# Moving the convolution of one group and the loads of its x to other bundles of a fused convolution and channel-mix kernel

## The chip, the cores and the metric

The kernel runs on one core of a Trainium2 chip. The metric is the device time of one launch in microseconds, as a median of several runs. A profile is one further execution, recorded by the hardware.

## What is computed

A lightweight convolution over time is followed by an RWKV channel mix. With batch 8, sequence 4160, width 192, 8 heads of 24 channels, 7 taps and hidden width 1024:

```python
w = softmax(weight, axis=-1)                                  # 8 heads x 7 taps
y[b, t, h*24 + c] = sum_k w[h, k] * x_pad[b, t + k, h*24 + c] # 6 zero rows ahead of x
y_prev = y shifted by one row
xk = mu_k * y + (1 - mu_k) * y_prev
xr = mu_r * y + (1 - mu_r) * y_prev
k = relu(xk @ w_k)                                            # 192 -> 1024
v = (k * k) @ w_v                                             # 1024 -> 192
out = sigmoid(xr @ w_r) * v
```

## The kernel before

**Work units.** The eight batches are taken as four pairs. A pair's 4160 rows are cut into steps of 512 rows (some of 256), and a step's first product, 192 to 1024, into slots. Four slots make a bundle. There are 260 slots and 65 bundles, 0 to 64. Pair 0 has bundles 0 to 15, pair 1 has 16 to 31, pair 2 (the third) 32 to 47, pair 3 the rest. A full step takes two bundles.

**A bundle** (`bundle_rest`, L938) writes out by hand what each engine does. TensorE computes four slots of k (`k_mm`, L593, 6 matmuls each), one r product (L650, 12 matmuls) and one v product (L681, 64 matmuls in two halves). ScalarE does a relu for each slot (L605) and a sigmoid (L661). VectorE squares the four slots (L619), multiplies r and v (L697), and makes the mixes of a later step (`diff` L536, `scale` L567, `add_y` L573). Where the bundle has a convolution unit, it comes after the fourth slot of k and before the second half of v.

**The convolution** is done ahead of the steps that need it, in groups of rows. Groups 0 to 7 belong to pairs 0 and 1. Groups 8 to 12 are "sparse": 20 blocks of 4 x 26 rows, 2080 rows, of two batches. Group 8 is the second half of pair 1, group 9 the first half of pair 2, groups 10, 11, 12 follow. A sparse group passes through these stages:

- `x_tile` and `load_x`: x goes from HBM into tile `xb`, cast to bf16, by DMAs from the GpSimd (POOL) queue, one batch at a time. The first batch goes in one bundle and the second in a later one, at the bundle's beginning (table `early`). A batch of group 9 is 4 DMAs of L154 and a small one of L148. A write of one word by VectorE (L125 in `x_tile`, L113 in `tie_x`) goes ahead of each batch and ties the load to its place. `x_tile` of group 9 also has one GpSimd memset (L127). `xb` has two buffers: group 9 takes the one of groups 6 and 7, which were convolved in bundles 7, 9, 11 and 12.
- `conv_sparse` (L350): four units, one for each two heads. A unit takes two tiles from the PSUM ring, runs 32 matmuls (L364), and ScalarE casts the two tiles into the two halves of `y` (L337), in 2 instructions for units 0 and 3 and in 4 for units 1 and 2.
- `y_write` (L466): 8 DMAs from the SP queue write `y` to `y_dram` at the end of the bundle of the last unit. `y` has two buffers and a sparse group uses both, so the casts of the next sparse group wait until these 8 DMAs have landed.
- `y_read` (L488): transposing DMAs from the SP queue bring `y_dram` into `yT`, which the mixes read. SP also issues the output stores (L705), two a bundle, and works through all of this in program order.

**The PSUM ring** has four tiles, shared by the k, r and v products and the convolution. A bundle without a unit takes six tiles and one with a unit takes eight.

**Where each group's stages stand** is worked out from `fb`, the bundle in which its rows are first needed, with exceptions in two small dictionaries (L752 and L760). Before the change, around the place in question:

| group | fb | x loaded in | convolved in | y written at the end of | y read at the end of |
|---|---|---|---|---|---|
| 7 | 20 | 7 | 11, 11, 12, 12 | 12 | 15 |
| 8 | 24 | 9, 12 | 14, 15, 16, 17 | 17 | 19, 22 |
| 9 | 32 | 17, 18 | 22, 23, 24, 25 | 25 | 27, 30 |
| 10 | 40 | 24, 25 | 27, 29, 31, 33 | 33 | 35, 38 |
| 11 | 48 | 29, 32 | 35, 37, 39, 41 | 41 | 43, 46 |
| 12 | 56 | 37, 40 | 43, 45, 47, 49 | 49 | 51, 54 |

Of the kernel before, what the change touches and what calls it, by code (L numbers as in the profile page):

```python
# [14 lines left out]
def kernel(  # L15
# [719 lines left out]
    def at(table, b, fn, *a):  # L735
        table.setdefault(b, []).append((fn, a))
# [7 lines left out]
    for g, (p, base, nb, fb, on_pe) in enumerate(groups):  # L744
        if g < 3:
            continue
        if p == 0:
            xs = {3: [1, 1], 4: [2, 2, 3, 3], 5: [4, 4, 5, 5]}[g]
        elif g not in sparse:
            xs = [fb - 9] * 2 + [fb - 7 - (g == 7)] * 2  # L750
        else:
            xs = {8: [14, 15, 16, 17], 9: [22, 23, 24, 25]}.get(g, [fb - 13, fb - 11, fb - 9, fb - 7])  # L752
        for i, b in enumerate(xs):
            xt.setdefault(b, []).append((g, i))
        if not on_pe:
            at(late, xs[-1], y_write, g)
        if g in sparse:
            at(late, max(fb - 5, xs[-1] + 2), y_read, g, slice(0, 1), 2)
            at(late, fb - 2, y_read, g, slice(1, 2), 2)
            b, b1 = {8: (9, 12), 9: (17, 18), 10: (24, 25)}.get(g, (fb - 19, fb - 16))  # L760
            at(early, b, x_tile, g)
            at(early, b, load_x, g, (0,))
            b = b1
            at(early, b, tie_x, g, 1)
            at(early, b, load_x, g, (1,))
            continue
        if not on_pe:
            if g == 4:
                at(mix_c, 4, y_read, g, slice(0, 1), 2)
                at(late, 4, y_read, g, slice(1, 2), 2)  # L770
            else:
                at(late, {5: 6, 6: 11, 7: 15}[g], y_read, g)
        if g > 4:

            b = {5: 1, 6: 3, 7: 7}.get(g)
            b = first_bundle[first_step[p]] + (-15, -11, -7, -3)[(g - 6) % 4] if b is None else b
            table = {5: mix_a, 7: mix_c}.get(g, early)
            at(table, b, x_tile, g)
            at(table, b, load_x, g)
    for s, (p, t0, L, n0, ns) in enumerate(steps):  # L780
        fb = first_bundle[s]
# [27 lines left out]
    for s, j, vb in quads:  # L809
        b = vb - (s == LAST)  # L810
# [261 lines left out]
```

## Time and profile before

| | us |
|---|---|
| median of 3 runs | 411.97 (411.53 to 412.25) |
| the profiled execution | 411.43 |
| its span, first to last instruction | 409.7 |
| around the span | 1.73 |
| granted TensorE clock | 1.0 |

| engine | busy us | share of the span |
|---|---|---|
| TensorE matmul (PE) | 401.9 | 98% |
| TensorE weight load (PEld) | 303.6 | 74% |
| VectorE (DVE) | 371.0 | 91% |
| ScalarE (ACT) | 354.6 | 87% |
| GpSimd (POOL) | 58.8 | 14% |

In what follows a bundle's start is the start of its first k matmul (L593) in the trace. Some of these, in us from the span's start: bundle 15 at 102.19, 16 at 108.53, 17 at 114.87, 18 at 121.18, 19 at 126.90, 22 at 144.10, 25 at 162.96, 27 at 175.02, 38 at 240.94, 43 at 271.25, 51 at 319.05. A window between two starts is the time that the program takes for the bundles between them. An idle time in square brackets names what ended it; "issue" means that the engine waited for nothing that the profile shows.

### The profile page before, as it was taken

To read this page: it belongs to the slowest core of one execution; us is meant where nothing else is said; L and a number is where in the kernel's file an instruction comes from. 1 tells how busy PE (TensorE), PEld (TensorE's weight loads), DVE (VectorE), ACT (ScalarE), POOL (GpSimd) and SP (SyncE) were. 2 spreads that over 40 slices of the span, in tenths; PEclk is the share of its full clock that TensorE was granted. 3 is DMA by queue.
4 is the path that set the end of the run, shared out by engine and by line. 5 is a ranking of instruction groups with operands and counts; after the bars stand their busy time and mean duration, and the time that the engine had idled before them with its cause. 6 is when DMAs were issued, how large, how long until landed. Compare 5 with 4: busy or idle time off the path is not lost.

```text
span 409.7 us, 17419 instructions
## 1 busy us (share of the span) xinstructions
PE 401.9 (98%) x7672; PEld 303.6 (74%) x7672; DVE 371.0 (91%) x672; ACT 354.6 (87%) x426; POOL 58.8 (14%) x91
## 2 busy tenths in 40 slices
PE   8899999999999999999999999999999999999996
PEld 5567767767867777777777777777777778777795
DVE  5899899998989999989999998999999899999973
ACT  6899988898998889998898898889898878877781
POOL 8632022030060004104020012000000002000000
PEclk9999999999999999999999999999999999999999
DMA  9999889997779977998995998979523756221223
GB/s 149 185 199 211 187 192 212 240 190 198 152 106 219 230 219 111 222 239 160 199 164 138 203 205 125 163 187 193 134 78 88 210 136 157 79 70 50 80 78 117
DMA packets 139123, 66.35 MB, mean 162 GB/s; under 512 B 89364, under 2 KB 139048, under 8 KB 139048
## 3 DMA queue, kind: packets, MB, share of 16 engines
q1 hardware_dynamic: 95704, 48.32, 47.2%
q0 software_dynamic: 42544, 16.36, 34.6%
q8 instruction: 60, 0.98, 1.0%
q10 hardware_dynamic: 800, 0.57, 0.5%
q14 instruction: 15, 0.12, 0.1%
HBM read 33.29 MB, written 36.99 MB: 172 GB/s over the span
## 4 chain that ended last, share of the span: by engine, by line
PE 93%; ACT 1%; issue 0%; DVE 0%; ACTq 0%
PE ps_v L681 41%; PE ps_k L593 39%; PE ps_r L650 8%; PE ps_c L364 2%; PE ps_v L633 1%; PE ps_c L319 1%; ACT k_sb L605 1%; ACT y L439 0%; PE ps_c L393 0%; DVE o_sb L717 0%; ACTq L401 0%; ACTq L605 0%
## 5 line engine op out<-in xcount | busy, mean ns | idle before, releaser
L605 ACT ACTIVATE k_sb<-ps_k 128x1024 bf16<-128x1024 f32 x260 | 253.4, 1040 | 34.2 <-PE ps_k L593 33.5
L619 DVE TENSOR_TENSOR k<-k_sb 128x1024 bf16<-128x1024 bf16 x260 | 173.4, 687 | 25.7 <-ACT k_sb L605 25.5
L593 PE MATMUL ps_k<-xk,wk 64*128 64x512 bf16 (+1 forms) x1632 | 191.8, 367 | 1.5 <-DMA wk<-in_moe_w_k_dram 1.4
L681 PE MATMUL ps_v<-wv,k 64*128 64x192 bf16 x4032 | 188.7, 243 | 0.3 <-issue 0.2
L681 PEld LDWEIGHTS <-k 64*128 64x128 bf16 x4032 | 168.6, 94 | 12.8 <-issue 5.1
L593 PEld LDWEIGHTS <-wk 64*128 64x128 bf16 x1632 | 83.8, 94 | 56.3 <-DMA wk<-in_moe_w_k_dram 1.9
L154 POOL DMA_DIRECT2D xb<-in_x_dram x62 | 43.7, 715 | 142.3 <-DVE xb L125 59.2
L697 DVE TENSOR_TENSOR o_sb<-ps_v,r_sb 128x768 f32<-128x768 f32 x64 | 60.8, 951 | 2.6 <-issue 2.4
L661 ACT ACTIVATE r_sb<-ps_r 128x768 bf16<-128x768 f32 x65 | 53.7, 828 | 9.0 <-PE ps_v L681 7.5
L337 ACT CAST y<-ps_c 128x960 bf16<-128x960 f32 (+2 forms) x84 | 52.6, 709 | 0.0
L650 PEld LDWEIGHTS <-xr 64*128 64x128 bf16 x780 | 34.8, 94 | 14.4 <-issue 0.4
L650 PE MATMUL ps_r<-wr,xr 64*128 64x192 bf16 x780 | 43.4, 243 | 0.0
L567 DVE TENSOR_SCALAR xr<-d,mu 128x512 bf16<-128x512 bf16 (+1 forms) x102 | 35.8, 355 | 0.0
L567 DVE TENSOR_SCALAR xk<-d,mu 128x512 bf16<-128x512 bf16 (+1 forms) x99 | 32.5, 359 | 0.1
L536 DVE TENSOR_TENSOR d<-yT 128x1536 bf16<-128x1536 bf16 (+4 forms) x36 | 31.2, 866 | 1.4 <-ACT yT L423 1.4
L573 DVE TENSOR_TENSOR xr<-xr,yT 128x1536 bf16<-128x1536 bf16 (+1 forms) x33 | 31.0, 938 | 1.1
L573 DVE TENSOR_TENSOR xk<-xk,yT 128x1536 bf16<-128x1536 bf16 (+3 forms) x33 | 30.5, 925 | 0.1
L520 POOL COPY y_tail<-yT 128x195 bf16<-128x195 bf16 x4 | 4.4, 1100 | 88.0 <-DMA yT<-y_dram 88.0
L364 PEld LDWEIGHTS <-toe 32*32 32x32 bf16 x640 | 4.4, 87 | 8.6 <-issue 7.4
L364 PE MATMUL ps_c<-xb,toe 32*32 32x240 bf16 x640 | 9.3, 267 | 0.0
L127 POOL MEMSET xb<- 32x384 bf16 x3 | 1.2, 408 | 55.3 <-DVE xb L125 55.3
L413 PE MATMUL ps_t<-toe,xb 128*32 128x120 bf16 (+3 forms) x264 | 5.6, 241 | 0.3 <-ACT xb L247 0.3
(60 smaller groups left out, 66.1 us busy)
## 6 DMA issues: line engine op xcount, KB each, us to landing
out_dram<-o_sb SPq DMA_DIRECT2D x128, 192.0 KB
xb<-in_x_dram POOLq DMA_DIRECT2D x52, 240.0 KB, 8.3
y_dram<-y SPq DMA_DIRECT2D x40, 195.0 KB
y_dram<-y SPq DMA_DIRECT2D x16, 210.0 KB
xb<-in_x_dram POOLq DMA_DIRECT2D x4, 228.0 KB, 4.8
xb<-in_x_dram POOLq DMA_DIRECT2D x4, 192.0 KB, 6.4
wk<-in_moe_w_k_dram POOLq DMA_DIRECT2D x4, 192.0 KB, 6.5
xb<-in_x_dram POOLq DMA_DIRECT2D x2, 216.0 KB, 4.9
```

The lines of the kernel that those rows point to most:

```text
L154: nc.gpsimd.dma_start(out=xb[q0 : q0 + rows, lo:hi, s, :], in_=bass.AP(tensor=x.tensor, offset=x.offset + (b * S + t0 + lo * step) * D, ap ...
L337: nc.scalar.copy(out=bass.AP(tensor=y.tensor, offset=y.offset + d, ap=[y.ap[0], [m * 2 * D, 2], [2 * D, m], [Q, 2], [1, b - a]],), in_=bas ...
L536: nc.vector.tensor_tensor(out=shaped(s, diffs[s][:, cs, :L]), in0=y_of(s, cs, 1), in1=y_of(s, cs, 0), op=ALU.subtract)
L567: nc.vector.tensor_scalar(out=t[:, c, :L], in0=diffs[s][:, c, :L], scalar1=mu[:, i, c : c + 1], scalar2=None, op0=ALU.mult)
L573: nc.vector.tensor_tensor(out=o, in0=o, in1=y_of(s, sl, 0), op=ALU.add)
L593: nc.tensor.matmul(out=ps[:, i, f * L : (f + 1) * L], lhsT=wk[r, c, fs], rhs=xk[r, c, :L], start=c == 0 and f == 0, stop=c == NC - 1 and f ...
L605: nc.scalar.activation(out=k_sb, in_=ps.rearrange("p a b -> p (a b)"), func=AF.Relu)
L619: nc.vector.tensor_tensor(out=o, in0=i, in1=i, op=ALU.mult)
L650: nc.tensor.matmul(out=ps[:, i, k * D : (k + 1) * D], lhsT=xr[q, c, ts], rhs=wr[q, c, :], start=c == 0, stop=c == NC - 1,)
L661: nc.scalar.activation(out=r_sbs[s, j], in_=r_ps.pop((s, j))[:, :, 0 : 2 * D], func=AF.Sigmoid)
L681: nc.tensor.matmul(out=v_ps[s, j][:, bank, k * D : (k + 1) * D], lhsT=k2s[s][q, f, t * P : (t + 1) * P], rhs=wv[q, f, :], start=half == 0 ...
L697: nc.vector.tensor_tensor(out=o_sb.rearrange("p (b t) d -> p b (t d)", b=2), in0=v_ps.pop((s, j)), in1=r_sbs.pop((s, j)), op=ALU.mult,)
```

## The change

Units 0, 1 and 2 of group 9 go from bundles 22, 23, 24 to bundles 19, 21, 23; unit 3 stays in bundle 25. With the exception at L752 gone, the rule `fb - 13, fb - 11, fb - 9, fb - 7` gives 19, 21, 23, 25. The first batch of its x is loaded in bundle 15 instead of 17, the second in bundle 16 instead of 18. Its `y_write` (bundle 25) and its `y_read`s (27 and 30) keep their places, and so does every stage of every other group.

```diff
         else:
-            xs = {8: [14, 15, 16, 17], 9: [22, 23, 24, 25]}.get(g, [fb - 13, fb - 11, fb - 9, fb - 7])
+            xs = {8: [14, 15, 16, 17]}.get(g, [fb - 13, fb - 11, fb - 9, fb - 7])
...
-            b, b1 = {8: (9, 12), 9: (17, 18), 10: (24, 25)}.get(g, (fb - 19, fb - 16))
+            b, b1 = {8: (9, 12), 9: (15, 16), 10: (24, 25)}.get(g, (fb - 19, fb - 16))
             at(early, b, x_tile, g)
             at(early, b, load_x, g, (0,))
             b = b1
             at(early, b, tie_x, g, 1)
             at(early, b, load_x, g, (1,))
```

## The prediction

> **What bounds the kernel.** I read the page's busy shares and the summary of the chain that ended last first, then windows over single bundles.
>
> ```profile
> PE 401.9 (98%) x7672; PEld 303.6 (74%) x7672; DVE 371.0 (91%) x672; ACT 354.6 (87%) x426; POOL 58.8 (14%) x91
> ...
> PE 93%; ACT 1%; issue 0%; DVE 0%; ACTq 0%
> ```
>
> TensorE sets the end. The change adds and removes no matmul, so it can only alter the time that TensorE loses inside its "busy" share. The windows show this. First bundles 19 to 26 (columns: window, length, busy of PE, PEld, DVE, ACT, POOL, clock, DMA share, GB/s):
>
> ```profile
> 126.90:132.63 5.73, 5.73 (x106) 4.35 (x103) 5.28 (x10) 4.58 (x6) 0.00 (x0) 1.00 1.25 227
> ...
> 144.10:150.31 6.21, 6.21 (x138) 4.57 (x134) 6.10 (x10) 5.18 (x7) 0.00 (x0) 1.00 0.58 172
> 150.31:156.64 6.33, 6.33 (x136) 4.58 (x134) 5.67 (x13) 6.33 (x9) 0.29 (x1) 1.00 0.66 167
> 156.64:162.96 6.32, 6.32 (x138) 4.60 (x134) 5.89 (x12) 6.31 (x10) 3.18 (x6) 1.00 1.01 132
> ...
> sum 48.12, PE 48.12 PEld 35.93 DVE 44.51 ACT 43.36 POOL 5.46; mean PE 6.01 PEld 4.49 DVE 5.56 ACT 5.42 POOL 0.68
> ```
>
> A bundle without a unit takes 5.73, the first with one (22) 6.21, the next ones 6.33 and 6.32. In those ACT is busy for the whole bundle: four units in a row make ScalarE the bound. Now bundles 43 to 50, where group 12 has the same four units in every second bundle, as group 9 will have:
>
> ```profile
> 271.25:277.45 6.20, 6.20 (x137) 4.44 (x134) 5.81 (x11) 5.17 (x7) 0.00 (x0) 1.00 0.82 234
> ...
> 289.38:295.14 5.76, 5.76 (x104) 4.39 (x102) 5.29 (x9) 5.72 (x8) 0.00 (x0) 1.00 0.63 151
> ...
> sum 47.80, PE 47.80 PEld 35.58 DVE 44.21 ACT 43.38 POOL 0.00; mean PE 5.97 PEld 4.45 DVE 5.53 ACT 5.42 POOL 0.00
> ```
>
> The timeline of TensorE shows where the difference sits:
>
> ```profile
> 148.62 0.42 PE L364 MATMUL ps_c<-xb,toe 32*32 32x240 bf16 x32
> ...
> 154.81 0.57 PE L364 MATMUL ps_c<-xb,toe 32*32 32x240 bf16 x32
> ```
>
> The same 32 matmuls take 0.42 in bundle 22 and 0.57 in bundle 23, where the late sigmoid holds a tile of the PSUM ring that the unit's second half needs.
>
> **The change, part by part.**
>
> 1. Units 0 to 2 move. The work is the same, so I compare eight bundles with eight: 48.12 before, 47.80 in the pattern that it gets (47.80 also for group 10, bundles 27 to 34). That is **-0.32 us**, of which bundles 23 to 25 give 3 x 0.12 = 0.36 and two bundles after a unit with four casts give 2 x 0.04 back (5.76 for 5.72). Bundle 19 has a unit two bundles after bundle 17, as 27 has after 25 (6.20). The VectorE work of a bundle depends on its parity, and 19, 21, 23 are odd like 27 to 33.
>
> 2. The x loads move two bundles ahead: 10 DMAs, two words written by VectorE (0.06 each) and a memset of POOL (0.41). POOL is idle for 26.94 before the memset, and nothing else stands in its queue between bundles 14 and 17, so its own order costs nothing. The words cost VectorE 0.06 in bundles 15 and 16 and save as much in 17 and 18: nothing. The `xb` buffer has been free since bundle 12. In the trace the loads are issued at 114.58 to 123.36 and the last has landed at 139.34 (by the semaphore updates). Now they are issued some 12.7 us earlier (bundle 15 starts that much before 17), about 102 to 110.5. The slowest last batch was 18.7 us from first issue to landing (120.62 to 139.34), which gives 107.8 + 18.7 = 126.5. Bundle 19's unit needs it at 126.90 + 4.5 = 131.4 (22's began 4.5 after its start). The margin falls to 5 us; without it each late us is an us of TensorE.
>
> 3. What the loads run into. Queue lines (start, duration of the issue):
>
> ```profile
> 104.70 3.85 SPq L488 DMA_TRANSPOSE yT<-y_dram  x1
> ...
> 121.38 7.15 SPq L466 DMA_DIRECT2D y_dram<-y  x8
> ...
> 134.48 7.44 SPq L488 DMA_TRANSPOSE yT<-y_dram  x1
> ```
>
> The read of group 7 (104.70) now lies between the two load batches. Alone it landed 5.8 us after its issue (110.54); group 6's, with a load beside it, took 10.1 (80.51 to 90.56). If both batches went ahead of it, it would land at 126.5, the bound of step 2. Its reader is the `diff` of bundle 18:
>
> ```profile
> 124.93 0.96 DVE L536 TENSOR_TENSOR d<-yT 128x1536 bf16<-128x1536 bf16 x1
> ```
>
> So between 110.5 and 126.5 against 124.93: nothing at the near end, 1.6 us at the far one. I take 10.1, the nearest row: 114.8, nothing. Behind the read on SP stand the output stores of bundle 16; a read of 7.44 instead of 3.85 delays them by 3.6, and four `o_sb` buffers at one a bundle cover 17 us.
>
> Here a rule speaks against the change. The Trainium skill, DMA: Bandwidth & Descriptors, "Issuing engines are not separate DMA queues", says that DMAs of SP and GpSimd end on the same 16 engines and interleave; the row of 10.1 against 5.8 agrees. By the rule the sum would still be -0.32 here, since the reader is later than either.
>
> 4. A new wait: the unit-0 casts of group 9 move from bundle 22 to 19 and must wait for the 8 writes of group 8, issued from 121.38. They landed at 138.34, beside the x loads. With no load at all group 10's writes took 11.0 us (217.41 to 228.41), with a load ending in their first 4.5 us group 9's took 10.6 (169.47 to 180.09). The second cast comes at about 133.6 (in bundle 19 the last relu ends at 132.68, one cast takes 0.95). So 132.4 against 133.6, nothing, if the loads are over by 126; at the far end 138.34, 4.7 us late. Queued behind on ScalarE are the relus of bundle 20, for which TensorE waits; ScalarE idles 1.16 in such a bundle (0.82 and 0.34), so the price ends at 3.5. I take nothing: the load ends as early as group 9's did.
>
> 5. TensorE's own instructions come by DMA (queue q8, 60 packets of 16 KB). By the packet records, the next packet usually starts when the 256 instructions before are 205 used; beside heavy DMA it starts later. The latest was at 241.0, 404 used, and only there does TensorE run dry:
>
> ```profile
> 243.43 0.17 PEld L650 LDWEIGHTS <-xr 64*128 64x128 bf16 x4 [0.23 <-issue]
> ...
> 250.72 0.34 PEld L681 LDWEIGHTS <-k 64*128 64x128 bf16 x8 [0.39 <-issue]
> ```
>
> Bundles 38 and 39 take 12.62, 36 and 37 take 11.92: 0.70 for it. At 37.5 instructions a us (15372 in 409.7), 404 - 205 is 5.3 us late. Beside loads alone (121.5) a packet was 4.4 late, beside a transposing read alone (143.2) 3.9, both without a stall. Now both run at once while packets are due at 106.2, 112.1 and about 117.5. Cost: from nothing to 8.3 - 5.3 = 3.0 us if the two delays add up. I take nothing, since group 11's load with group 9's read behind it (packet at 197.7, 219 used) made none late; both ends stay in the range.
>
> The Trainium skill, Runtime: NRT & Kernel Launch, "Instruction fetch mechanics", says that instructions are refilled in blocks of 256 and that crossing a block is mostly hidden. The stall at 243 differs; by the rule the sum is -0.32, by the stall's row -0.32 + 0.70 = +0.38.
>
> **Sum.** -0.32 against the profiled execution: span 409.38, time 411.11. The median of the runs stands 0.54 above that execution (411.97 to 411.43), and I carry the difference over: **411.65**, -0.08%. A measurement of this kernel can tell about 0.2% (0.8 us) from no change.
>
> **Rivals.**
>
> - *Slower: TensorE starves in bundles 16 to 18* (step 5), from the point where a packet is over 5.3 us late. For it: loads and a read never overlap fully in the trace, and each alone comes within 1.5 us of the limit. Against it: no packet but one passed it. Price 0.70 to 3.0, total 412.3 to 414.7, in the middle 413.5.
> - *Slower: ScalarE waits for the writes of group 8 in bundle 19* (step 4; steps 2 and 3 would add to it), if the loads outlast 126. Total 411.65 to 415.2, in the middle 413.4.
> - *Faster by more*: the stall of bundles 38 and 39 is chance and doesn't come again, or packets that were 4.4 and 3.9 late at 121.5 and 143.2 did stall in unprofiled runs (whose median is 0.54 higher) and now don't. -0.32 - 0.70: 410.95.
> - *It does nothing*: ScalarE's backlog only moves, since group 8's four units in a row (14 to 17) stay. Bundle 18 is back at 5.73, which speaks against it. 411.97.
>
> **How the numbers follow.** Forecast 0.35 and "does nothing" 0.08, both within 0.2%: 0.43. Faster 0.24. Starving TensorE by enough 0.22 and ScalarE's wait 0.11: slower 0.33. Cases of all signs hold much, so the forecast's own range is 411.2 to 412.4 (a stall of 0.70 included at the top). For 8 in 10 the range takes in the faster case (410.95, and 0.15 below it, half of the forecast's own gain) and the slower ones past their middles: 410.8 to 413.9.
>
> **What would show it.** Right: bundles 19 to 26 sum to 47.8, every L364 there takes 0.42, no bundle with a unit takes 6.33. Wrong: gaps "issue" on L681 or L593 in 104 to 125; `diff` of bundle 18 waiting for `yT`; L337 in bundle 19 starting after 133; L364 of bundle 19 waiting for `xb`. Bundles 38 and 39 at 12.6 or at 11.9 decide the third rival.

## The result: slower by 0.4%, and the profile after

Over 13 runs each, the changed kernel takes 413.19 us (median) and the kernel before 411.60. The ratio is 1.0044, with a 95% interval of 1.0029 to 1.0060. The profiled execution of the changed kernel took 412.11, its span 410.40: 0.70 more than the span of before (409.70). The three slowest of the changed kernel's 13 runs (414.99 to 415.11) had a granted clock of 0.994 to 0.996 and the other ten 0.998 to 1.000, with a median of 412.99, so that the slower clock isn't what makes the difference.

The page of the changed kernel shows hardly anything: TensorE's busy time is even a little lower, and 1% of the chain is now "issue".

```profile
PE 401.5 (98%) x7672; PEld 303.6 (74%) x7672; DVE 370.4 (90%) x672; ACT 354.6 (86%) x426; POOL 58.7 (14%) x91
...
PE 93%; ACT 1%; issue 1%; DVE 0%; ACTq 0%
```

Windows over bundles find the place. Bundles 17, 18 of the kernel before (columns as in the prediction), then 17, 18 of the changed one:

```profile
114.87:121.18 6.31, 6.31 (x137) 4.60 (x135) 5.66 (x13) 6.30 (x9) 4.19 (x7) 1.00 0.84 113
121.18:126.90 5.72, 5.72 (x104) 4.30 (x102) 5.28 (x9) 5.49 (x7) 2.18 (x4) 1.00 1.49 209
```

```profile
114.93:121.84 6.91, 6.42 (x137) 4.57 (x135) 5.33 (x11) 6.18 (x9) 0.00 (x0) 1.00 1.51 154
121.84:128.50 6.66, 5.90 (x104) 4.51 (x102) 5.20 (x9) 5.55 (x7) 0.00 (x0) 1.00 1.12 271
```

They lose 0.60 and 0.94, and TensorE is no longer busy throughout (6.42 of 6.91 us, 5.90 of 6.66). The timeline of its weight loads in these two bundles:

```profile
118.84 0.50 PEld L681 LDWEIGHTS <-k 64*128 64x128 bf16 x12 [0.72 <-issue]
...
125.86 0.67 PEld L681 LDWEIGHTS <-k 64*128 64x128 bf16 x16 [0.99 <-issue]
```

Two gaps in the middle of a v product, with nothing that the profile shows to wait for. Counted from TensorE's first instruction, they lie before instructions 4546 and 4802: exactly 256 apart, both 194 after a multiple of 256. The gaps of the kernel before in bundles 38 and 39 lie before 9410 and 9666, 194 after a multiple of 256 too. TensorE's instructions come in packets of 16 KB, each with a block of 256, so I take these places for the boundaries of blocks; a run below tests it.

The queue lines show what stands beside them: the read of group 7, and the `diff` that needs it.

```profile
104.89 9.13 SPq L488 DMA_TRANSPOSE yT<-y_dram  x1
```

```profile
125.52 0.96 DVE L536 TENSOR_TENSOR d<-yT 128x1536 bf16<-128x1536 bf16 x1
```

The read now takes 9.13 us to issue instead of 3.85 and lands at 122.08 (by the semaphore updates), 17.2 after its start instead of 5.8. Its reader comes at 125.52 and still doesn't wait.

The forecast gain is there as well. Bundles 21 to 23 and the sum of 19 to 26:

```profile
140.48:146.68 6.20, 6.20 (x137) 4.44 (x134) 5.81 (x11) 5.17 (x8) 0.00 (x0) 1.00 0.21 69
146.68:152.44 5.76, 5.76 (x105) 4.39 (x102) 5.30 (x9) 5.72 (x8) 0.00 (x0) 1.00 0.64 155
152.44:158.66 6.22, 6.22 (x139) 4.58 (x135) 5.82 (x12) 5.20 (x8) 0.27 (x1) 1.00 0.44 119
...
sum 47.85, PE 47.85 PEld 36.08 DVE 44.26 ACT 43.43 POOL 5.58; mean PE 5.98 PEld 4.51 DVE 5.53 ACT 5.43 POOL 0.70
```

48.11 has become 47.85, and no bundle of these takes 6.33 any more. The account of the two profiled executions: +1.54 in bundles 15 to 18, -0.26 in 19 to 26, -0.64 in 38 and 39 (no gap this time), +0.06 ahead of bundle 3: +0.70.

### The profile page after: what moved, and what is told of

Same layout as the page of the kernel before. It is cut to its first block, busy times and chain, and to the rows that moved or that the text cites. A ratio compares the mean times of both kernels' runs of the same rounds, so it can differ in the third digit from the quotient of the medians.

```text
span 410.4 us, 17419 instructions
## 1 busy us (share of the span) xinstructions
PE 401.5 (98%) x7672; PEld 303.6 (74%) x7672; DVE 370.4 (90%) x672; ACT 354.6 (86%) x426; POOL 58.7 (14%) x91
## 4 chain that ended last, share of the span: by engine, by line
PE 93%; ACT 1%; issue 1%; DVE 0%; ACTq 0%
PE ps_v L681 41%; PE ps_k L593 39%; PE ps_r L650 8%; PE ps_c L364 2%; PE ps_v L633 1%; PE ps_c L319 1%; ACT k_sb L605 1%; ACT y L439 0%; PE ps_c L393 0%; DVE o_sb L717 0%; ACTq L401 0%; ACTq L605 0%
```

## The experiments

The theory: TensorE's instruction packets come late while the loads of group 9 share the DMA engines with the transposing read of group 7, and TensorE runs dry at the end of a block. Rivals: the new places of the units cost; the loads alone are enough; TensorE waits for a semaphore (a signal of another engine) or for late data. Each run's ratio is to the kernel before on the same chip. Sums are between the bundles' first k matmuls, in us of the run's profiled execution.

| run | ratio (95% interval) | 15 to 18 | 19 to 26 | 30 to 33 | 38, 39 |
|---|---|---|---|---|---|
| before | | 24.71 | 48.11 | 23.95 | 12.61 |
| changed | 1.0044 (1.0029 to 1.0060) | 26.25 | 47.85 | 23.95 | 11.97 |
| e1_loads_only | 1.0057 (1.0032 to 1.0082) | 25.69 | 48.18 | 23.95 | 12.39 |
| e2_read7_late14 | 1.0000 (0.9983 to 1.0016) | 25.69 | 47.80 | 23.95 | 11.98 |
| e3_loads_13_14 | 1.0054 (1.0034 to 1.0075) | 26.76 | 47.80 | 24.03 | 12.19 |
| e4_loads_15_17 | 1.0029 (1.0010 to 1.0049) | 26.25 | 48.17 | 24.89 | 13.28 |
| e5_load11_29_30 | 1.0046 (1.0018 to 1.0074) | 25.24 | 48.16 | 25.23 | 12.50 |
| e6_shift_blocks | 1.0166 (1.0131 to 1.0201) | 26.99 | 47.85 | 23.95 | 11.97 |
| e7_read14_loads_15_17 | 1.0017 (0.9994 to 1.0040) | 25.50 | 47.85 | 23.94 | 13.99 |
| e8_read14_units_21 | 1.0018 (0.9997 to 1.0039) | 25.31 | 48.06 | 24.04 | 12.48 |
| e9_loads_18_19 | 1.0074 (1.0043 to 1.0106) | 24.71 | 53.30 | 23.95 | 12.19 |
| e10_changed_again | 1.0026 (1.0002 to 1.0050) | 28.18 | 47.85 | 24.08 | 12.47 |
| e11_read14_again | 1.0021 (0.9998 to 1.0044) | 25.61 | 47.80 | 24.62 | 13.54 |
| e12_before_again | one execution: 410.81 us | 24.71 | 48.11 | 23.94 | 11.97 |

### The loads alone

```diff
-            b, b1 = {8: (9, 12), 9: (17, 18), 10: (24, 25)}.get(g, (fb - 19, fb - 16))
+            b, b1 = {8: (9, 12), 9: (15, 16), 10: (24, 25)}.get(g, (fb - 19, fb - 16))
```

> The kernel before with only the loads of group 9 moved (bundles 15 and 16); its units stay in bundles 22 to 25. Theory (TensorE's instruction packets come late while these loads and the transposing read of group 7 share the DMA engines): bundles 17 and 18 take 13.0 to 13.8 us as in the changed kernel (13.57) instead of 12.04, with issue gaps on L681 256 instructions apart, and bundles 19 to 26 stay at 48.1; the time is 1.2 to 2.2 us above the kernel before (ratio 1.003 to 1.005). Rival (the new places of the units cost, by ScalarE's casts or the ring): bundles 17 and 18 take 12.04 and the ratio is 1.000.

```profile
125.14 0.67 PEld L681 LDWEIGHTS <-k 64*128 64x128 bf16 x16 [0.99 <-issue]
```

The gap stands before the same instruction 4802 as in the changed kernel, the read again takes 17.4 us, and the ratio is the changed kernel's within the intervals. So moving the loads is enough for the slowdown, and the units' new places aren't needed for it. That rival is out.

### The read ahead of the loads

The changed kernel with:

```diff
-                at(late, {5: 6, 6: 11, 7: 15}[g], y_read, g)
+                at(late, {5: 6, 6: 11, 7: 14}[g], y_read, g)
```

> The changed kernel with the read of group 7 issued at the end of bundle 14 instead of 15, so that most of it lies ahead of the loads. Theory: the read lands within about 7 us and by 107, no packet comes with over 360 instructions used in bundles 15 to 19, bundles 17 and 18 are back at 12.04, bundles 19 to 26 take 47.8; the time is 0.2 to 0.8 below the kernel before (ratio 0.998 to 0.9995). Rival (the loads alone delay the packets, as many of them follow each other; the read doesn't matter): bundles 17 and 18 stay above 13 and the ratio is 1.003 to 1.005.

> The changed kernel with the read of group 7 at the end of bundle 14, once more and beside the run ahead. Theory: the read lands by 106 and the sum of gaps in bundles 16 to 19 is 0.4 to 1.3 us, 0.8 to 1.5 less than in the changed kernel; ratio 0.998 to 1.002. Rival (the loads alone set the gaps): the same gaps as the changed kernel and the same ratio.

In the first of the two runs the read starts at 98.91 and takes 3.03 to issue; it lands at 105.47, 2.4 us after the first of the large load DMAs was issued (103.04).

```profile
98.91 3.03 SPq L488 DMA_TRANSPOSE yT<-y_dram  x1
```

```profile
112.69 0.34 PEld L681 LDWEIGHTS <-k 64*128 64x128 bf16 x8 [0.80 <-issue]
...
119.16 0.50 PEld L681 LDWEIGHTS <-k 64*128 64x128 bf16 x12 [0.39 <-issue]
```

Bundles 19 to 26 take 47.80 as expected, but 15 to 18 still lose 0.98, and 0.90 in the repetition, at block boundaries (instructions 4290 and 4546). The gaps come long after the read has landed, so the loads, with the other traffic of these bundles, are enough for a part of the slowdown, as the rival had it.

That the read beside the loads brings the rest is likely, but not shown. Where the read lies ahead, bundles 15 to 18 lose 0.98, 0.90 and 0.79 (e7). Where it meets the loads they lose 1.54 and 3.47 (the two profiles of the changed kernel), 2.05 (e3), 1.54 (e4) and 2.28 (e6), but in e1 only 0.98, no more than in e2. By time, e2 lies clear below the changed kernel (1.0000 against 1.0044, intervals apart), while e11 and e10, run side by side, can't be told apart (1.0021 and 1.0026).

### Other places for the loads

In the changed kernel, and then in the kernel before:

```diff
-9: (15, 16)
+9: (13, 14)
...
-9: (17, 18)
+9: (15, 17)
```

> The changed kernel with the loads of group 9 in bundles 13 and 14, so that they lie ahead of the read of group 7, which stays. Theory: the overlap with the read is only the tail of the second batch, bundles 17 and 18 take 12.04, bundles 19 to 26 take 47.8, ratio 0.998 to 0.9995; a gap in bundles 13 to 15 is possible because group 7 writes y there. Rival (new places of the units cost): ratio above 1.003 whatever the loads do.

> The kernel before with the first batch of group 9 loaded in bundle 15 and the second in 17 as the first was; units stay in 22 to 25. A dose: the read of group 7 overlaps one batch instead of two. Theory: the read takes 9 to 13 us instead of 17, a packet near 108 to 113 starts with 300 to 360 used, no gap or one under 0.3 us, ratio 0.9990 to 1.0015. Rival (it is the first batch that delays the packets): bundles 16 to 18 lose over 0.7 us, ratio 1.002 to 1.005.

Both missed. With the loads in 13 and 14 the second batch, beside the writes of group 7, wasn't over before the read but lasted until 118.03 (21.3 us from its first issue), the read took 15.0, and two gaps of 0.92 and 1.18 followed. With 15 and 17 the read still took 14.4 (105.05 to 119.41), and gaps of 1.26 and 0.44 followed. It met the whole first batch (103.29 to 116.30) and, from 114.43 on, the beginning of the second, so this run wasn't the half dose that it was meant to be.

### The same collision elsewhere

In the kernel before, group 9 untouched:

```diff
-10: (24, 25)}
+10: (24, 25), 11: (29, 30)}
```

> The kernel before, with the same kind of collision made in another place: the second batch of group 11's x is loaded in bundle 30 instead of 32, so that the transposing read of group 9 at the end of bundle 30 starts among loads. Group 9 keeps its places. Theory (loads beside a transposing read make TensorE's instruction packets late): the read takes over 12 us instead of 7.3, and bundles 30 to 33, 23.95 us before, take 24.5 to 25.7, with issue gaps 256 instructions apart; ratio 1.001 to 1.004. Rival (the slowdown belongs to group 9's place, its units or the writes of group 8): bundles 30 to 33 stay within 0.1 of 23.95 and the ratio is 1.000.

```profile
196.56 10.61 SPq L488 DMA_TRANSPOSE yT<-y_dram  x1
```

```profile
211.94 0.69 PEld L681 LDWEIGHTS <-k 64*128 64x128 bf16 x17 [1.09 <-issue]
```

The read takes 15.0 instead of 7.3, and bundles 30 to 33 lose 1.28. So a loss of this kind doesn't need group 9's place, its units or the writes of group 8. How much of the 1.28 the moved load makes is less sure than it looks: e4 and e11 leave this place as it was, and there the same four bundles lost 0.94 and 0.67, in one gap at a block boundary each (see the table). Of the rest of what this profile lost, 0.53 came in bundle 18, where the kernel is the one before.

### Moving the block boundaries

The changed kernel with 128 more TensorE instructions in front:

```diff
-    SHORT = 78
+    SHORT = 142
```

> The changed kernel with 142 instead of 78 tiny matmuls at the very beginning, while TensorE waits for its first data: 128 more instructions on TensorE, so that every later instruction stands half a block of 256 further on. Theory: the issue gaps stay at the same place of a block (194 instructions after a multiple of 256, counted from the first) and so move 128 instructions within the program, from L681 in bundles 17 and 18 to other instructions about 3.5 us earlier or later; the loss in bundles 15 to 19 is 0.5 to 2 us and the ratio 1.001 to 1.006. Rival (a semaphore, or data that come late for one instruction): the gaps stay at the same instructions of L681.

```profile
124.80 0.32 PEld L364 LDWEIGHTS <-toe 32*32 32x32 bf16 x32 [0.42 <-issue]
125.28 0.53 PEld L681 LDWEIGHTS <-k 64*128 64x128 bf16 x14 [0.15 <-issue]
128.13 0.75 PEld L681 LDWEIGHTS <-k 64*128 64x128 bf16 x18 [2.33 <-issue]
```

The gap of bundle 17 has gone from the first half of v (after 20 weight loads) past the convolution into the second half (after 14): 12 + 6 + 32 + 14 = 64 weight loads and as many matmuls, 128 instructions. Counted from the first instruction it is before 4801, so at the same place of a block. A semaphore or late data would have stayed with its instruction; that rival is out. The ratio says nothing of bundles 15 to 18, since the edit cost 5.4 us before bundle 3, which I hadn't expected. The trace shows where: TensorE sat idle for 3.06 us up to 15.63, within two instructions of a block boundary by the same count (before 704; the packet began at 13.31), beside the first loads of x and the weights, and from 14.82 to 21.65 its granted clock was 0.5.

### Trying for a better version

First the changed kernel with the read in 14 and the loads in 15 and 17; then the kernel before with the read in 14 and units in 21, 23, 24, 25; then the kernel before with the loads in 18 and 19:

```diff
-9: (15, 16)
+9: (15, 17)
...
-9: [22, 23, 24, 25]
+9: [21, 23, 24, 25]
...
-9: (17, 18)
+9: (18, 19)
```

> The changed kernel with the read of group 7 at the end of bundle 14 and the loads in bundles 15 and 17, so that the read and the two batches follow each other with the least overlap. Theory: from one block's end to the start of the next packet 2.5 to 4.2 us, gaps in bundles 15 to 20 sum to under 0.6, bundles 19 to 26 take 47.8, ratio 0.998 to 1.000. Rival (loads beside the dense bundles 15 to 17 are enough, whatever the read does): gaps of 1 us and more, ratio 1.000 to 1.003.

> The kernel before with the read of group 7 at the end of bundle 14, and unit 0 of group 9 in bundle 21 instead of 22, unit 1 in 23, unit 2 in 24, unit 3 in 25; its loads stay in 17 and 18. No load meets a read more than before. Theory: bundles 19 to 26 take 47.9 to 48.0 (one 6.33 less in the row), no new gaps, ratio 0.998 to 1.001. Rival (the new places of units cost more than the windows show): ratio above 1.002.

> The kernel before with the loads of group 9 one bundle later, in 18 and 19 instead of 17 and 18; units stay in 22 to 25. Bundles 18 to 21 have no unit, so that a block of 256 instructions lasts about 7.0 us there instead of 6.0 in bundles with units. Theory (a gap comes when a packet's delay is over the block's length less 2.4 us): no gap in bundle 18 (the kernel before has one of 0.6 us in some executions), but the second batch now meets the read of group 8 at 134, so that bundles 19 to 21 may lose 0 to 1; ratio 0.998 to 1.002. Rival (the number of loads beside the read decides, not the block's length): bundles 19 to 22 lose 1.2 us and more, ratio above 1.003.

The first two are inconclusive by time (both intervals take in 1). Their gaps in bundles 15 to 18 sum to 0.84 (0.25 and 0.59) and 0.65, and 38 and 39 lost 2.0 in the first. The third missed by another mechanism, the one that my step 3 had priced: the read of group 8 met the second batch, took 18.2, and its reader came first.

```profile
152.38 0.96 DVE L536 TENSOR_TENSOR d<-yT 128x1536 bf16<-128x1536 bf16 x1 [3.85 <-DMA yT<-y_dram]
```

VectorE waited 3.85, and bundles 22 and 23 took 4.94 more. A part of that is not the wait: TensorE idled until 155.73, and from 155.87 to 159.28 its granted clock was 0.50. No version beat the kernel before.

### The same kernels again

> The changed kernel once more, for a second profile and to stand beside the next run on one chip. Theory: gaps on TensorE in bundles 16 to 19 at 194 instructions after a multiple of 256, 1.2 to 2.5 us in sum; bundles 19 to 26 at 47.8; ratio 1.003 to 1.006. Rival (the first profile's gaps were chance): no gaps there, ratio 0.999.

> The kernel before, a second profile. Theory: gaps at the ends of blocks are chance near the limit: 0 to 0.7 in bundle 18 and 0 to 2 in bundles 38 and 39, with everything else as in the first profile. Rival (they belong to the schedule): the same 0.70 in 38 and 39 and none in 18.

The changed kernel again has its gaps before 4546 and 4802, and one of them is the largest of all. The loss in bundles 15 to 18, 3.47, is above the 1.2 to 2.5 that I expected of its gaps:

```profile
120.69 0.50 PEld L681 LDWEIGHTS <-k 64*128 64x128 bf16 x12 [3.19 <-issue]
...
127.16 0.67 PEld L681 LDWEIGHTS <-k 64*128 64x128 bf16 x16 [0.44 <-issue]
```

The kernel before has none in bundles 38 and 39 this time (12.61 in the first profile):

```profile
sum 11.97, PE 11.97 PEld 8.95 DVE 11.10 ACT 10.90 POOL 0.00; mean PE 5.99 PEld 4.47 DVE 5.55 ACT 5.45 POOL 0.00
```

Over the fourteen profiles, none of which touches what bundles 38 and 39 do, these two lose between 0 and 2.0. Each of the two kernels that were profiled twice without an edit has it once and once not. So this stall comes and goes from one execution to the next; a single profile can't tell a change of it from chance.

## Why the prediction was wrong

- **The gain (step 1) was right**: -0.32 forecast, -0.26 measured in both profiles of the changed kernel, and -0.31 where bundle 19 isn't disturbed by what lies before it (47.80 in three runs). The 32 matmuls of a unit take 0.42 in bundles 19, 21, 23 and 25, as in bundle 22 before. But -0.3 of 412 is less than what a late packet can cost (gaps up to 3.19).
- **The loads (step 2) were right**: the last landed at 126.95 (126.5 forecast), the unit of bundle 19 didn't wait for them.
- **The read of group 7 (step 3): the size failed.** I took 10.1 from the one row with a load beside it; it took 17.2. It landed at 122.08, nearer to the far bound of 126.5 than to the 114.8 that I took. The reader at 125.52 was spared by 3.4 us, so this cost nothing by itself, but it made loads and read overlap for 17 us.
- **The writes of group 8 (step 4) were right**: landed at 133.08, and the first casts of bundle 19 began at 134.10 without a wait.
- **TensorE's instructions (step 5) is the step that failed.** It named the mechanism and the bundles, priced it between 0 and 3.0, and then took nothing; the profiles show 1.54 and 3.47 there. Two things were wrong.
  - *The limit.* I put it at 5.3 us late, from the packet of 241.0, by counting instructions and turning 404 - 205 = 199 of them into time at the mean rate of 37.5 a us. In that stretch, which has a unit, TensorE was faster: it passed the boundary at 237.12, so the packet of 241.03 came 3.91 us after it. It is better to measure from the other end. At every gap at a block boundary in bundles 15 to 18, over all profiles, the packet starts 2.2 to 2.9 us before TensorE can go on, most often about 2.4. A block lasts 6.1 us where bundles have units (kernel before, the block that ends in bundle 18) and 7.3 in the next. So a packet may start some 3.7 us after the boundary before it in the one and 4.9 in the other. At the place of bundle 18's gap the packet came 3.41 and 2.91 late in the two profiles of the kernel before, without a gap; 4.38 and 4.46 in e5 and e8, with gaps of 0.58 and 0.65; and 4.58 in the changed kernel, with 0.99. The packet before the gap of 3.19 came 6.49 late.
  - *The row weighed against it.* Group 11's load with group 9's read behind it overlapped for 3.5 us (195.79 to 199.31) and not for 17. And that it made no packet late was true of one execution: in e4 and e11 this same place, not edited, lost 0.94 and 0.67.
- The 0.70 that I charged for the stall of bundles 38 and 39 is two late packets and not one, since its gaps (0.23 and 0.39) stand at two boundaries. The second profile puts the two bundles at 11.97 without it, so that it cost 0.64.
- The rule on instruction fetch (the Trainium skill, Runtime: NRT & Kernel Launch, "Instruction fetch mechanics"), that crossing a block is mostly hidden, fits most of the 60 blocks of a profile here, but not all of those beside the loads: there the measurement decides, with gaps up to 3.19 us.
- **Of the rivals**, the first came true in bundles 17 and 18, at +1.54 and +3.47 beside its price of 0.70 to 3.0; its total in the middle (413.5) is near the measured 413.19, which is in part luck, with single executions so far apart. "Faster by more" was built on a stall that comes and goes: each kernel has it in one of its two profiles. The 0.54 that I carried over from three runs was chance as well: over 13 runs the median of the kernel before is 411.60, 0.17 above its profiled execution.

What stays open: why a packet beside the same DMAs is 2.9 late in one execution and 4.4 in another (the kernel before and e5, which is the same up to there), and how much of a packet's delay is the load's, the read's and the output stores'. No run took one of them away altogether, since the kernel needs all. That the packets wait for room on the DMA engines is inferred from their lateness beside the loads; the traces don't show what a packet waits for.

## What to carry to other kernels

When TensorE is the bound, with tens of instructions a microsecond, its instruction stream is one more transfer with a due time: count the instructions between a packet and the end of its block, and treat heavy DMA stretches as risks to TensorE even where every data transfer has slack. In this kernel a transposing read should not start among the loads, since each lengthened the other (read 5.8 to 17.2 us, second batch 11.5 to 18.6). Take a second profile of the same kernel before reading a difference of this size out of one. An expected gain of tenths of a microsecond should be set against what the schedule loses at one stroke, here one late packet (0.25 to 3.19 us).

## What the runs showed of the hardware that I hadn't expected

- Gaps of TensorE marked "issue" before instructions that are multiples of 256 apart, moving by 128 instructions when 128 are put in front: 0.25 to 3.19 us each in bundles 15 to 18.
- The read of group 7 lands 5.8 us after its start without loads beside it and 14.4 to 18.1 with them; group 9's 7.3 after its start behind a load and 15.0 among loads (e5), group 8's 11.0 and, with a batch of loads beside it for 15 us, 18.2 (e9). Its issue on SP grows from 3.85 to 9.13, and group 8's from 7.44 to 14.20.
- A batch of x loads takes 10.5 us from its first issue to its last landing where no read or write of y runs beside it (253.20 to 263.65 in the kernel before). The second batch of group 9 takes 11.5 in e2, with the read ahead (108.50 to 120.01), 18.6 beside the read in the changed kernel, and 21.3 beside writes and the read in e3.
